# Attention and two MLP blocks on one core: heads on all rows of the array, fewer load issues, a new list of steps, weight subtractions on VectorE

## Chip, cores and metric

One core of a Trainium2 chip. The metric is the device time of one execution in microseconds (us), lower is better. Engines by their names in the profile: PE = TensorE matmul, PEld = its weight loads, DVE = VectorE, ACT = ScalarE, POOL = GpSimd, SP = SyncE; SPq is the queue on which SP issues transfers (DMA).

## What is computed

Windowed attention (batch 4, 8 heads, 576 tokens, head size 64; heads 0 to 3 see the last 32 tokens, heads 4 to 7 every fourth of the last 128), then two MLP blocks over 2304 tokens of width 512. All is float32.

```python
scores = q @ k.T / sqrt(64); scores = where(mask, scores, -1e9)
attn = exp(scores - max); attn = attn / (sum(attn) + 1e-9)
x = attn @ v                                  # then to [2304, 512]
h = x @ w_in;  x = (h - tanh(h)) @ w_out      # w_in [512, 2048], w_out [2048, 512]
out = ((x @ w1) * (x @ w2)) @ w3 @ w_out2     # w1, w2 [512, 1024], w3 [1024, 1024], w_out2 [1024, 512]
```

## The kernel before

**Attention.** The work is cut into 12 units (a batch and a third of its tokens) and two types of heads, plain (p) and dilated (d), whose tokens the host has put into residue order so that both types use the same narrow windows. A type of a unit is a part here, so there are 24. A part has two pairs of heads (e) and three blocks of 64 tokens (i). Each part goes through these steps, named by one letter in the list:

- q: load of k and q (`load_q`, L295). k is one issue (L306); q is four issues (L313), one for each pair and head, each the 64 rows of one head. The type takes one half of the 128 rows (`r`).
- v: load of v (`load_v`, L322, L333), 2 issues or, for the first third of a batch, 4.
- s: scores (`at_scores`, L371). A matmul of identity and mask opens the bank (L389); then 24 matmuls of 64 rows, 32 columns of weights (q) and 64 moving columns (k) add to it (L402), each two instructions in the trace. The four column strips of the array are two heads by two halves of a block. Units 0 to 2 run one type at a time; from unit 3 on `s3` and its like run both, each on its half of the rows.
- M, E, N, m: maximum and subtraction (DVE), exponential (ACT), sum and reciprocal (DVE), product (POOL).
- T: three transposes by PE (L447); C: their copy to SBUF (ACT, L455).
- P: weighted sum of v (`at_pv`, L458, L476): 24 matmuls of 64 rows by 64 weight columns and 32 moving columns.
- X, L: the high part of the result on ACT (L498) and the rest on DVE (L503), written to X.

**First block.** A float32 product is computed from high and low parts by three matmuls. Its 16 chunks of 128 hidden columns are in four groups of 3, 4, 4 and 5. Steps: h (`st_h`: x @ w_in), t, g, G, k (tanh, subtraction, high, low), y (`st_y`: product with w_out), Y, Z (to SBUF). A step of 256 tokens has 12 matmuls for h and 12 for y. The first group runs beside the attention, in the order that `ORDER` (L45) writes out by hand for all engines at once: every engine and SP's queue get their instructions in the order of the words, and wait in that order. `S5` is five matmuls on zeros. The words h0 to h24 are the steps of h; h24 is the first of group 1, from where loops give the order.

**Weights** arrive as 64-bit words and are turned into float32 high and low parts: w (load, `load64`), a (L126, ACT), b and c (L131, L135, L141, L144, DVE), i (high, `cv_hi`, ACT), o (low, `cv_lo`, L152, POOL). Outside the list `tick` (L188) does this for one weight; `need` calls it until a weight is there; two staging buffers hold arriving words. Converted weights take free slots (`free`), which `release` and `settle` give back two steps later.

**Second block.** First `WW` = w3 @ w_out2, 8 steps of 24 matmuls (L739). Then for tiles of 512 tokens and 8 chunks j: `st_ab` (two products of 12 matmuls each, pa and pb; a_sb from pa by ACT, L777; the product with pb by DVE, L778; cs high by ACT, L780, cs low by DVE, L781), and `st_out` of the step before (L797, 12 matmuls that need cs). In the first tile every step calls `tick` twice after `st_ab`. `y_split` (L726) makes the high and low parts of the next tile's input, on ACT and DVE.

Of the kernel before, what the change touches and what calls it, by code (L numbers as in the profile page):

```python
# [50 lines left out]
t2 C3p q5 g2 i4 b5 T3d G2 o4 h3 c5 C3d k2 P3 M4 i5 t3 q6 o5 y1 X3p X3d L3p E4 L3d y2 N4 s5 Y2 Z2 m4p
v5d g3 m4d G3 T4p v5p M5 k3 h4 C4p q7 T4d E5 s6 C4d N5 t4 P4 g4 m5p M6 G4 q8 y3 m5d X4p X4d k4 T5p
L4p E6 L4d s7 C5p N6 v6p T5d m6p h5 C5d M7 m6d q9 T6p t5 P5 g5 E7 s8 X5d N7 X5p G5 C6p k5 L5p v7d y4
L5d m7d v7p m7p T6d w6 h6 C6d M8 w7 T7p t6 y5 g6 E8 q10 G6 N8 a6 h7 k6 Y5 Z5 C7p m8p s9 a7 b6 m8d t7
v6d g7 T7d c6 G7 h8 k7 C7d q11 M9 i6 T8p t8 o6 y6 g8 E9 b7 y7 G8 N9 k8 w8 h9 c7 m9d m9p P6 t9 w9 i7
g9 y8 X6p o7 X6d v8p L6p C8p L6d h10 G9 v8d Z8 Y8 k9 a8 y9 a9 b8 t10 c8 P7 s10 b9 X7p w10 X7d L7p
g10 v9d T8d L7d G10 h11 c9 k10 C8d v9p M10 P8 t11 a10 w11 y10 X8d X8p L8d v10p E10 g11 s11 L8p G11
v10d N10 k11 h12 b10 m10p c10 m10d y11 t12 g12 w12 T9p Z11 G12 h13 Y11 k12 C9p y12 t13 g13 G13 T9d
k13 h14 C9d M11 P9 t14 g14 E11 T10p v11p h15 X9p N11 C10p v11d G14 X9d k14 T10d L9p t15 y13 L9d m11p
C10d g15 m11d P10 G15 k15 h16 X10p X10d L10p L10d T11p t16 y14 g16 C11p T11d Z14 G16 h17 Y14 k16  # L60
C11d y15 t17 g17 P11 G17 k17 y16 X11p X11d L11p L11d Q0 h18 i8 i9 o8 y17 t18 i10 g18 o9 G18 a11 h19
# [7 lines left out]
def attn_moe_kernel(  # L69
# [276 lines left out]
    def banks_of(n, ty):  # L346

        if n >= PB:
            s = ust[n]
            return s["both"][:, ty], lambda: s["xt"][:, ty]  # L350
        m = order0.index((n, ty))
        if 2 <= m < 4:

            ps = yA.tile([128, 2, 256], F32, tag=f"y{m - 2}", name=f"s{m}").rearrange("p a c -> p (a c)")
        else:
            if m % 4 == 0:
                banks0["s"] = attn_pools["psS"].tile([128, 2, 512], F32, tag="s", name="s")
            ps = banks0["s"][:, m % 2]

        def x():  # L360
            if m % 2 == 0:
# [542 lines left out]
```

## Time and profile before

| | us |
|---|---|
| median of 3 runs | 870.97 |
| lowest, highest | 868.84, 871.27 |
| the profiled execution | 869.45 |
| its span, first to last instruction | 867.7 |

| engine | busy us | share of the span |
|---|---|---|
| PE | 825.8 | 95% |
| PEld | 693.8 | 80% |
| DVE | 430.1 | 50% |
| ACT | 277.9 | 32% |
| POOL | 139.2 | 16% |

The shares are means over stages that differ; the section of rows below splits the span into stages. The clock of a row is the share of full speed that TensorE was granted: 1.00 is 2.4 GHz, 0.50 is 1.2 GHz. A busy PE is not always PE at its peak, since a matmul counts as busy from its start to its modelled end.

### The profile page before, as it was taken

The numbers are of one execution on the slowest core, as the hardware profiler recorded it, in microseconds if no ns is written. First come the engines' busy times: TensorE is split into PE (matmuls) and PEld (weight loads), VectorE is DVE, ScalarE is ACT, GpSimd is POOL, SyncE is SP. The second block draws the span as 40 slices with busy tenths as digits, with TensorE's granted clock in tenths as the row PEclk, the third lists the DMA queues.
The fourth block names the chain that finished last, engine by engine and source line by source line (L and its number), as shares of the span: only waits on it lengthen the run. The fifth ranks groups of instructions, "written<-read, shape, count | busy, mean of one in ns | idle before, by whom it ended". The sixth has DMA issues, their size and how long they took to land.

```text
span 867.7 us, 14652 instructions
## 1 busy us (share of the span) xinstructions
PE 825.8 (95%) x6153; PEld 693.8 (80%) x6153; DVE 430.1 (50%) x728; ACT 277.9 (32%) x507; POOL 139.2 (16%) x136
## 2 busy tenths in 40 slices
PE   7878859999999999999999999999899999999998
PEld 3577658988888988888888898887688888888897
DVE  4566447465763576335776776766722222222121
ACT  2333234544432243223444433334321121121121
POOL 3232222351210021001222211222100000000000
PEclk9588969999999999999999999999999999999999
DMA  6675567121220022002232222323010010010010
GB/s 155 176 215 130 124 174 229 43 74 48 97 74 1 25 97 74 1 1 67 89 103 98 96 83 74 104 91 122 25 49 1 1 48 1 1 49 0 1 49 25
DMA packets 49250, 63.18 MB, mean 73 GB/s; under 512 B 23072, under 2 KB 37536, under 8 KB 49184
## 3 DMA queue, kind: packets, MB, share of 16 engines
q1 hardware_dynamic: 48896, 61.88, 23.7%
q8 instruction: 48, 0.79, 0.4%
q10 hardware_dynamic: 288, 0.36, 0.2%
q14 instruction: 18, 0.15, 0.1%
HBM read 57.51 MB, written 4.72 MB: 72 GB/s over the span
## 4 chain that ended last, share of the span: by engine, by line
PE 79%; SPq 7%; DMA 5%; DVE 4%; ACT 2%; issue 2%; POOL 0%; ACTq 0%; DVEq 0%; POOLq 0%
PE h L519 46%; PE y L609 21%; PE o L797 10%; SPq L313 4%; SPq L333 2%; DMA st<-in_w 2%; PE x L476 1%; SPq L306 1%; DMA st<-in_w_out 1%; DMA st<-in_w_in 1%; DMA v<-in_vt 1%; DMA Y<-in_kT 1%; DVE a L141 1%; DVE a L135 1%; DVE a L144 1%
## 5 line engine op out<-in xcount | busy, mean ns | idle before, releaser
L609 PE MATMUL y<-gs,WG 128*128 128x512 f32 (+1 forms) x648 | 125.3, 342 | 0.1
L519 PE MATMUL h<-X,WG 128*128 128x256 f32 (+1 forms) x591 | 122.6, 343 | 1.9 <-DVE th L567 1.9
L519 PE MATMUL h<-X,LT 128*128 128x512 f32 (+1 forms) x552 | 122.1, 368 | 0.0
L567 DVE TENSOR_TENSOR th<-h,th 128x512 f32<-128x512 f32 (+1 forms) x83 | 51.3, 618 | 131.1 <-ACT th L561 130.9
L519 PE MATMUL h<-LT,X 128*128 128x512 f32 (+1 forms) x402 | 115.9, 373 | 0.0
L609 PEld LDWEIGHTS y<-gs,WG 128*128 128x128 f32 x648 | 104.2, 194 | 13.3 <-POOL gs L581 0.3
L519 PEld LDWEIGHTS h<-X,LT 128*128 128x128 f32 x552 | 96.7, 189 | 17.3
L519 PEld LDWEIGHTS h<-X,WG 128*128 128x128 f32 x591 | 95.9, 198 | 13.7 <-DVE th L567 2.5
L778 DVE TENSOR_TENSOR a_sb<-h,a_sb 128x512 f32<-128x512 f32 (+1 forms) x40 | 25.5, 637 | 158.7 <-PE h L519 152.4
L609 PE MATMUL y<-gs,LT 128*128 128x512 f32 (+1 forms) x420 | 93.4, 368 | 0.9 <-DVE gs L581 0.9
L561 ACT ACTIVATE th<-h 128x512 f32<-128x512 f32 (+1 forms) x83 | 44.8, 540 | 137.7 <-PE h L519 137.6
L609 PEld LDWEIGHTS y<-gs,LT 128*128 128x128 f32 x420 | 74.1, 188 | 14.1 <-DVE gs L581 1.1
L519 PEld LDWEIGHTS h<-LT,X 128*128 128x128 f32 x402 | 73.5, 188 | 13.3
L519 PE MATMUL h<-WG,X 128*128 128x512 f32 (+1 forms) x225 | 69.2, 375 | 0.0
L574 ACT ACTIVATE gs<-th 128x512 fp32r<-128x512 f32 (+1 forms) x83 | 47.8, 576 | 60.7 <-DVE th L567 56.7
L141 DVE SCALAR_TENSOR_TENSOR a<-st,a 128x512 uint32<-128x512 uint32 x72 | 60.4, 839 | 2.2
L126 ACT ACTIVATE a<-st 128x512 f32<-128x512 f32 x72 | 47.8, 664 | 41.9 <-DMA st<-in_w_in 20.2
L152 POOL TENSOR_TENSOR WG<-a,WG 128x512 fp32r<-128x512 f32 x27 | 35.1, 1298 | 141.0 <-ACT WG L149 125.6
L144 DVE SCALAR_TENSOR_TENSOR a<-st,a 128x512 uint32<-128x512 uint32 x72 | 54.0, 750 | 2.5
L797 PE MATMUL o<-X,cs 128*128 128x512 f32 x216 | 52.6, 391 | 1.9 <-ACT cs L780 1.9
L777 ACT ACTIVATE a_sb<-h 128x512 f32<-128x512 f32 (+1 forms) x40 | 22.0, 551 | 94.2 <-PE h L519 94.2
L780 ACT ACTIVATE cs<-a_sb 128x512 fp32r<-128x512 f32 (+1 forms) x40 | 23.6, 589 | 87.9 <-DVE a_sb L778 87.9
(84 smaller groups left out, 1013.2 us busy)
## 6 DMA issues: line engine op xcount, KB each, us to landing
st<-in_w SPq DMA_DIRECT2D x32, 512.0 KB, 3.3
st<-in_w_in SPq DMA_DIRECT2D x16, 512.0 KB, 3.5
st<-in_w_out SPq DMA_DIRECT2D x16, 512.0 KB, 3.6
v<-in_vt SPq DMA_DIRECT2D x28, 192.0 KB, 3.8
st<-in_wo SPq DMA_DIRECT2D x8, 512.0 KB, 3.2
q<-in_qz SPq DMA_DIRECT2D x72, 48.0 KB, 2.9
k<-in_kT SPq DMA_DIRECT2D x12, 224.0 KB, 3.8
v<-in_vt SPq DMA_DIRECT2D x14, 128.0 KB, 3.8
```

Source lines behind the costliest of these rows:

```text
L126: nc.scalar.activation(out=a.bitcast(F32), in_=st[:, :, 1].bitcast(F32), func=ACTF.Abs)
L141: nc.vector.scalar_tensor_tensor(out=a, in0=st[:, :, 1], scalar=0xC0000000, in1=a, op0=ALU.bitwise_and, op1=ALU.bitwise_or)
L144: nc.vector.scalar_tensor_tensor(out=a, in0=st[:, :, 0], scalar=29, in1=a, op0=ALU.logical_shift_right, op1=ALU.bitwise_or)
L152: nc.gpsimd.tensor_tensor(out=lo, in0=a.bitcast(F32), in1=hi.bitcast(F32), op=ALU.subtract)
L313: nc.sync.dma_start(out=q[r, e, h], in_=qz[b, 2 * ty + e, D * h:D * h + D, TU * g:TU * g + TU, QT * h:QT * h + QT],)
L519: nc.tensor.matmul(out=ps, lhsT=a[sel[0]], rhs=b[sel[1]], start=(start and i == 0), stop=(i == n - 1), **kw)
L561: nc.scalar.activation(out=th[:, :tn], in_=gst[i][:, :tn], func=ACTF.Tanh)
L567: nc.vector.tensor_tensor(out=th[:, :tn], in0=ps[:, :tn], in1=th[:, :tn], op=ALU.subtract)
L574: nc.scalar.activation(out=gs[:, 0, :tn], in_=th[:, :tn], func=ACTF.Copy)
L609: nc.tensor.matmul(out=y[k], lhsT=wt[sel[0]][:, 128 * k:128 * k + 128], rhs=gs[:, sel[1], tn * m:tn * m + tn], start=(cs[m] == 0 and n == ...
L778: nc.vector.tensor_tensor(out=a_sb[:, :tn], in0=pb[:, :tn], in1=a_sb[:, :tn], op=ALU.mult)
L797: nc.tensor.matmul(out=ps, lhsT=cs[:, e, 128 * m:128 * m + 128], rhs=WW[j][f], start=(j == 0 and n == 0), stop=(j == NJ - 1 and n == 2),)
```

## The change

- Loads: a part has its own k and q tiles on all 128 rows, one issue for each. q is now loaded with its zero blocks (128 rows: one head's rows hold q, the other's zeros, in the columns of each head), 384 KB instead of four times 48 KB. Three buffers for k and q (before, two of a whole unit), three for v (four).
- Scores: 24 matmuls a part of 128 rows, 32 weight columns, 64 moving columns; the four column strips as before, no half of rows for a type any more.
- C: the transposed weights go to a tile `pb` that holds blocks on a diagonal (pair e in rows 64 e and on), in two ACT instructions of 64 rows; its zeros are written once by two POOL memsets at the start.
- P: 12 matmuls a part of 128 rows (both pairs), 64 weight columns, 64 moving columns. Its PSUM tile is one bank, two buffers (before, one of two banks).
- A new list for the first group; q, v and P come by part everywhere. M, E and N stay for both types at once from unit 3 on.
- From WW on (`late`), the low part of weights is computed by DVE; a weight's steps are spread around the evacuation in `st_ab`; WW takes one or two weights a step; in the first tile, two weights in the first two steps, then one. `y_split` is cut in two (`y_hi`, `y_lo`).

```diff
--- before.py
+++ after.py
-q0p S10 v2p K0 q2p K1 s0p w0 S5 M0p q1p E0p s2p N0p q0d S3 a0 m0p M2p T0p b0 E2p q1d C0p s1p N2p c0
-m2p S1 v0p s0d M1p i0 w2 S1 o0 M0d E1p s1d v1p N1p E0d P0p w1 M1d m1p S1 X0p a2 T1p q2d L0p N0d S3
...
+q0p S10 q1p K0 K1 q1d s0p S2 M0p q2p s1p E0p N0p S6 v1p M1p m0p T0p E1p q0d S1 C0p N1p s2p m1p v0p
+M2p T1p S4 C1p q2d E2p s0d N2p s1d m2p v0d M0d P0p E0d M1d w0 P1p X0p N0d E1d T2p w1 X1p N1d m0d s2d
+C2p L1p m1d L0p T0d v2p M2d a0 S5 C0d v1d b0 E2d T1d c0 a1 q3p S2 P2p N2d i0 P0d o0 b1 X2p w2 C1d S6
+X0d q3d L2p m2d L0d P1d c1 T2d X1d v2d a2 L1d i1 b2 h0 C2d w3 o1 c2 s3 t0 q4p g0 i2 P2d M3 G0 o2 q4d
+a3 h1 X2d k0 b3 E3 y0 w4 t1 c3 v3p g1 i3 s4 L2d G1 o3 N3 v3d a4 k1 h2 M4 w5 m3p m3d T3p t2 v4p g2
+C3p b4 h3 G2 q5p c4 E4 P3p t3 a5 g3 k2 T3d N4 X3p v4d h4 i4 C3d o4 L3p q5d b5 t4 P3d y1 g4 m4d X3d
+c5 v5p h5 G3 q6p L3d m4p i5 s5 k3 o5 t5 w6 g5 T4p M5 y2 q6d C4p P4p Y2 Z2 E5 q7p T4d y3 C4d N5 X4p
+v5d P4d G4 m5p L4p G5 a6 m5d T5p v6p X4d b6 s6 C5p k5 c6 w7 T5d P5p M6 k4 q7d C5d y4 X5p i6 L5p E6
...
-        nc.gpsimd.tensor_tensor(out=lo, in0=a.bitcast(F32), in1=hi.bitcast(F32), op=ALU.subtract)
+        (nc.vector if late else nc.gpsimd).tensor_tensor(out=lo, in0=a.bitcast(F32), in1=hi.bitcast(F32), op=ALU.subtract)
...
+    def conv_bits():
+        if absed and len(free) - (reserve[0] if absed[0][0][0] in ("w1", "w2") else 0) >= 2:
+            key, st, a = absed.popleft()
+            cv_bits(st, a)
+            late[0] = key, a, free.popleft(), free.popleft()
+        prefetch()
+        if loaded and not absed:
+            key, st = loaded.popleft()
+            absed.append((key, st, cv_abs(st)))
+
+    def conv_hi():
+        if late[0]:
+            cv_hi(late[0][1], late[0][2])
+
+    def conv_lo():
+        if late[0]:
+            key, a, hi, lo = late[0]
+            cv_lo(a, hi, lo)
+            W[key] = (hi, lo)
+            late[0] = None
+
+    def tick_late():
+
+
+        conv_lo()
+        conv_bits()
+        conv_hi()
+
...
-                tick()
+                tick_late() if late else tick()
...
-        attn_pools["kv"] = st.enter_context(tc.tile_pool(name="kv", bufs=2))
-        attn_pools["vv"] = st.enter_context(tc.tile_pool(name="vv", bufs=4))
+        attn_pools["kv"] = st.enter_context(tc.tile_pool(name="kv", bufs=3))
+        attn_pools["vv"] = st.enter_context(tc.tile_pool(name="vv", bufs=3))
...
-        attn_pools["pt"] = st.enter_context(tc.tile_pool(name="pt", bufs=4))
+        one = st.enter_context(tc.tile_pool(name="att", bufs=1))
+        attn_pools["pb"] = one.tile([128, NPB, TU, 4, 2, HQ], F32, name="pb")
...
-        attn_pools["psX"] = st.enter_context(tc.tile_pool(name="psX", bufs=1, space=PSUM))
+        attn_pools["psX"] = st.enter_context(tc.tile_pool(name="psX", bufs=2, space=PSUM))
+
+        for e in range(2):
+            nc.gpsimd.memset(attn_pools["pb"][64 * e:64 * e + 64, :, :, :, 1 - e], 0.0)
...
-            if n not in ks:
-                k = home(n, 4 * WK, "kv", "k").rearrange("p (m k) -> p m k", m=4)
...
             for ty in parts:
-                r = slice(64 * ty, 64 * ty + 64)
+                k = home(n, 2 * WK, "kv", "k").rearrange("p (e k) -> p e k", e=2)
+                q = home(n, 2 * TU * 2 * QT, "kv", "q").rearrange("p (e t c) -> p e t c", e=2, t=TU)
                 nc.sync.dma_start(
-                    out=k[r, :, :k1 - k0],
-                    in_=kT[b, 2 * ty:2 * ty + 2, :, k0:k1].rearrange("e (h p) k -> p (e h) k", h=2),
+                    out=k[:, :, :k1 - k0], in_=kT[b, 2 * ty:2 * ty + 2, :, k0:k1].rearrange("e p k -> p e k")
                 )
-                for m in range(4):
-                    e, h = divmod(m, 2)
-
-                    nc.sync.dma_start(
-                        out=q[r, e, h],
-                        in_=qz[b, 2 * ty + e, D * h:D * h + D, TU * g:TU * g + TU, QT * h:QT * h + QT],
-                    )
+                nc.sync.dma_start(
+                    out=q, in_=qz[b, 2 * ty:2 * ty + 2, :, TU * g:TU * g + TU].rearrange("e p t c -> p e t c")
+                )
+                ks[n, ty] = k, q
...
-        for i in range(TU):
-            t = TU * g + i
-            for e in range(2):
-                for ty in parts:
-                    r = slice(64 * ty, 64 * ty + 64)
+        for ty in parts:
+            k, q = ks.pop((n, ty))
+            for i in range(TU):
+                t = TU * g + i
+                for e in range(2):
                     for j in range(4):
-                        h, half = divmod(j, 2)
-                        k0 = KS[t] - KS[TU * g] + window(t, half)
+                        k0 = KS[t] - KS[TU * g] + window(t, j % 2)
                         nc.tensor.matmul(
-                            out=ps[ty][HQ * j:HQ * j + HQ, 2 * i + e],
-                            lhsT=q[r, e, h, i, HQ * half:HQ * half + HQ],
-                            rhs=k[r, 2 * e + h, k0:k0 + HW], start=False, stop=(i == TU - 1),
-                            skip_group_check=True, tile_position=(64 * ty, HQ * j),
+                            out=ps[ty][HQ * j:HQ * j + HQ, 2 * i + e], lhsT=q[:, e, i, HQ * j:HQ * j + HQ],
+                            rhs=k[:, e, k0:k0 + HW], start=False, stop=(i == TU - 1),
+                            skip_group_check=True, tile_position=(0, HQ * j),
                         )
...
-            pt = attn_pools["pt"].tile([128, TU, 128], F32, tag="p", name="p")
-            nc.scalar.activation(out=pt, in_=ust[n]["pt"][u], func=ACTF.Copy)
-            ust[n]["pt"][u] = pt
+            pt = ust[n]["pt"][u]
+            pb = ust[n]["pt"][u] = attn_pools["pb"][:, npb[0] % NPB]
+            npb[0] += 1
+            for e in range(2):
+                nc.scalar.activation(
+                    out=pb[64 * e:64 * e + 64, :, :, e],
+                    in_=pt[64 * e:64 * e + 64].rearrange("p i (j q) -> p i j q", j=4), func=ACTF.Copy,
+                )
...
-                for half in range(2):
-                    for e in range(2):
-                        for h in range(2):
-                            dst = x[64 * h:64 * h + 64, e]
-                            if ty:
-                                dst = dst[:, QT * i + HQ * half:QT * i + HQ * half + HQ]
-                            else:
...
-                            j = 2 * h + half
-                            nc.tensor.matmul(
-                                out=dst, lhsT=v[64 * e:64 * e + 64, half, i, D * h:D * h + D],
-                                rhs=s["pt"][ty][64 * e:64 * e + 64, i, HQ * j:HQ * j + HQ],
-                                start=True, stop=True, tile_position=(64 * e, 64 * h),
-                            )
+                for half, h in ((0, 0), (0, 1), (1, 0), (1, 1)):
+                    dst = x[64 * h:64 * h + 64]
+                    if ty:
+                        dst = dst[:, :, QT * i + HQ * half:QT * i + HQ * half + HQ]
+                    else:
+
+                        dst = dst.rearrange("p e (r c l) -> p c e l r", r=R, l=HQ // R)[:, 2 * i + half]
+                    nc.tensor.matmul(
+                        out=dst, lhsT=v[:, half, i, D * h:D * h + D],
+                        rhs=s["pt"][ty][:, i, 2 * h + half].rearrange("p a q -> p (a q)"), start=True, stop=True,
+                    )
+            s["x"][ty] = x
...
-        def y_split(t, k):
+        def y_hi(t, k):
             t0, tn = tiles[t]
-            ysp.setdefault(t, [])
             hi, lo = free.popleft(), free.popleft()
             nc.scalar.activation(out=hi[:, :tn], in_=Y[:, k, t0:t0 + tn], func=ACTF.Copy)
+            ysp.setdefault(t, []).append((hi, lo))
+
+        def y_lo(t, k):
+            t0, tn = tiles[t]
+            hi, lo = ysp[t][k]
             nc.vector.tensor_tensor(
                 out=lo[:, :tn], in0=Y[:, k, t0:t0 + tn], in1=hi[:, :tn].bitcast(F32), op=ALU.subtract
             )
-            ysp[t].append((hi, lo))
...
+        while bitsed:
+            split()
+        late.append(None)
...
             hi, lo = free.popleft(), free.popleft()
+            tick_late()
+            if i % 2:
+                tick_late()
             nc.scalar.activation(out=hi, in_=ps, func=ACTF.Copy)
-            tick()
...
+            if 2 <= i <= 5:
+                y_lo(0, i - 2)
             if 1 <= i <= 4:
-                y_split(0, i - 1)
+                y_hi(0, i - 1)
...
+            ny = j - 3 if 3 <= j < 7 and t + 1 < len(tiles) else None
+            if ny is not None:
+                y_hi(t + 1, ny)
+            conv_lo()
+            if t == 0:
+                conv_bits()
+            if ny is not None:
+                y_lo(t + 1, ny)
             a_sb = act_p.tile([128, 512], F32, tag="th", name="a_sb")
             nc.scalar.activation(out=a_sb[:, :tn], in_=pa[:, :tn], func=ACTF.Copy)
+            conv_hi()
             nc.vector.tensor_tensor(out=a_sb[:, :tn], in0=pb[:, :tn], in1=a_sb[:, :tn], op=ALU.mult)
             cs = spl_p.tile([128, 2, 512], F32R, tag="gs", name="cs")
             nc.scalar.activation(out=cs[:, 0, :tn], in_=a_sb[:, :tn], func=ACTF.Copy)
+            conv_lo()
             nc.vector.tensor_tensor(
                 out=cs[:, 1, :tn], in0=a_sb[:, :tn], in1=cs[:, 0, :tn].bitcast(F32), op=ALU.subtract
             )
+            if t == 0 and j < SECOND:
+                conv_bits()
+                conv_hi()
...
-                t, j = steps2[i]
-                if t == 0:
-                    tick()
-                    tick()
-                if j >= 3 and j < 7 and t + 1 < len(tiles):
-                    y_split(t + 1, j - 3)
...
```

## Rows read from the trace of the kernel before

**Rows 1.** Windows by stage: length, busy us of each engine (instructions), granted clock, DMA.
```profile
core 0: us, PE busy (x) PEld busy (x) DVE busy (x) ACT busy (x) POOL busy (x), PEclk, DMA share, GB/s
0.00:47.01 47.01, 37.28 (x684) 22.83 (x684) 23.25 (x54) 12.47 (x24) 12.68 (x25) 0.71 0.65 171
47.01:125.35 78.34, 57.10 (x1165) 50.70 (x1164) 43.55 (x75) 26.40 (x56) 22.46 (x25) 0.80 0.63 160
125.35:195.20 69.85, 67.90 (x1156) 62.78 (x1155) 40.06 (x72) 32.84 (x75) 27.82 (x29) 0.98 0.38 115
195.20:519.33 324.13, 323.26 (x1573) 273.81 (x1572) 194.48 (x335) 120.68 (x199) 50.74 (x40) 1.00 0.19 63
...
570.00:620.00 50.00, 46.11 (x200) 36.76 (x198) 37.18 (x54) 18.82 (x32) 12.90 (x10) 1.00 0.28 95
```

**Rows 2.** Waits of PE, 0 to 125 us: total, times, longest (us).
```profile
PE t L447 <- ACT p L455: 8.9, 3, 7.1
PE s L402 <- DMA q<-in_qz: 7.7, 10, 2.2
```

**Rows 3.** Chain that ended last, 0 to 118 us, by line.
```profile
by line: SPq L313 29.5%; SPq L333 14.7%; SPq L306 7.4%; DMA st<-in_w_out 6.3%; DMA st<-in_w_in 6.1%; DMA v<-in_vt 5.3%; DMA Y<-in_kT 5.3%; PE h L519 5.1%; issue 4.6%; DMA q<-in_qz 4.0%; PE x L476 2.9%; PE s L402 2.5%; SPq L121 2.5%; PE y L6
```

**Rows 4.** Time line of SP's queue: start, us, engine, line, issues.
```profile
62.58 0.61 SPq L306 DMA_DIRECT2D k<-in_kT  x1
63.23 3.33 SPq L313 DMA_DIRECT2D q<-in_qz  x4
```

**Rows 5.** DMA issues: count, KB each, us to landing.
```profile
v<-in_vt SPq DMA_DIRECT2D x28, 192.0 KB, 3.8
...
q<-in_qz SPq DMA_DIRECT2D x72, 48.0 KB, 2.9
```

**Rows 6.** Windows: scores of one type, of two; P of two; dense DMA.
```profile
15.90:17.10 1.20, 1.20 (x48) 0.99 (x48) 1.15 (x1) 0.02 (x1) 0.60 (x1) 1.00 0.23 55
...
61.65:62.80 1.15, 1.15 (x97) 1.09 (x96) 1.11 (x4) 1.12 (x3) 0.12 (x1) 1.00 0.64 186
...
126.90:128.40 1.50, 1.50 (x97) 1.46 (x96) 0.42 (x1) 0.90 (x2) 1.23 (x3) 1.00 0.58 163
26.00:30.00 4.00, 3.41 (x35) 1.91 (x35) 1.72 (x5) 1.93 (x4) 0.83 (x1) 0.50 0.98 304
```

**Rows 7.** Unit steps: chain at 152 us, mask matmuls, copy (x24, mean 487 ns).
```profile
152.87 0.33 PE t L447 x3
153.19 1.43 PE h L519 x12
...
61.23 0.49 PE L389 MATMUL s<-mask_sb,id_sb 128*128 128x384 bf16 x2
...
L455 ACT ACTIVATE p<-t 128x384 f32<-128x384 f32 x24 | 11.7, 487 | 16.1 <-PE t L447 16.1
```

**Rows 8.** First matmuls of h0, h9 (time line of PE) and h24 (chain).
```profile
47.01 1.67 PE L519 MATMUL h<-X,WG 128*128 128x256 f32 x12
...
125.35 1.60 PE L519 MATMUL h<-X,WG 128*128 128x256 f32 x12
...
195.20 2.72 PE h L519 x12
```

**Rows 9.** First tile of second block: PE's waits; DVE and POOL time lines.
```profile
PE o L797 <- ACT cs L780: 3.9, 2, 2.0
...
570.59 0.42 DVE L131 TENSOR_SCALAR a<-a 128x512 f32<-128x512 f32 x1
...
572.84 0.42 DVE L131 TENSOR_SCALAR a<-a 128x512 f32<-128x512 f32 x1
...
573.75 1.81 DVE L141 SCALAR_TENSOR_TENSOR a<-st,a 128x512 uint32<-128x512 uint32 x1
...
573.72 1.29 POOL L152 TENSOR_TENSOR X<-a,X 128x512 fp32r<-128x512 f32 x1 [7.55 <-ACT X L149]
...
502.11 0.69 DVE L581 TENSOR_TENSOR gs<-th,gs 128x512 fp32r<-128x512 f32 x1
```

More of the change, by code (lines that the diff above doesn't have):

```diff
@@ L16 @@
 PH = 1
+SECOND = 2
 GS = (3, 4, 4, 5)
@@ L51 @@
[L51 to L61, printed above, removed]
@@ new lines @@
+w8 o6 L4d h6 a7 N6 q8p y5 t6 b7 g6 m6d s7 c7 G6 Y5 v6d a8 Z5 k6 i7 w9 h7 b8 M7 m6p y6 q8d t7 o7 g7
+E7 T6p c8 h8 q9p G7 a9 N7 k7 C6p P5d t8 w10 b9 s8 X5d m7d L5d g8 v7p m7p c9 G8 y7 q9d k8 T6d a10 P6p
+C6d M8 q10p h9 X6p L6p E8 y8 b10 v7d t9 g9 P6d N8 G9 w11 Y8 k9 s9 X6d Z8 m8d L6d v8p m8p c10 T7p
+q10d h10 C7p P7p t10 q11p g10 T7d G10 X7p h11 k10 M9 C7d v8d T8p t11 P7d g11 E9 w12 L7p s10 X7d N9
+C8p v9p L7d m9p P8p m9d q11d T8d X8p y9 C8d L8p M10 v9d h12 G11 k11 E10 P8d t12 N10 s11 X8d v10p L8d
@@ new lines @@
+m10p g12 m10d h13 y10 t13 g13 y11 G12 k12 T9p Y11 Z11 h14 C9p G13 T9d k13 t14 y12 g14 C9d M11 y13
+G14 k14 E11 P9p N11 P9d X9p v10d L9p m11p T10p X9d h15 v11p C10p L9d m11d T10d t15 P10p g15 C10d y14
+X10p v11d G15 L10p k15 P10d Y14 Z14 T11p X10d h16 C11p L10d y15 t16 g16 G16 P11p k16 h17 X11p L11p
+y16 t17 g17 G17 h18 k17 y17 t18 g18 G18 T11d k18 Y17 Z17 h19 C11d P11d t19 g19 y18 X11d G19 L11d Q0
+k19 i8 h20 i9 o8 i10 y19 t20 o10 a11 g20 G20 b11 h21 k20 c11 y20 o9 t21 w13 i11 g21 o11 G21 h22 Z20
@@ L65 @@
+a12 Y20 k21 b12 a13 y21 t22 b13 g22 c12 G22 h23 k22 c13 i12 y22 t23 o12 i13 g23 G23 o13 h24 k23 y23
+t24 g24 G24 k24 Y23 Z23
 """
@@ L172, in attn_moe_kernel @@
     reserve = [0]
+    late = []
     loaded = deque()
@@ L226, in attn_moe_kernel @@
     AB = (0, 1)
+    NPB = 2
     Yf = Y.rearrange("p k n -> p (k n)")
@@ L344, in attn_moe_kernel, with bank_of @@
     banks0 = {}
-    def banks_of(n, ty):
+    def bank_of(n, ty):
         if n >= PB:
-            s = ust[n]
-            return s["both"][:, ty], lambda: s["xt"][:, ty]
+            return ust[n]["both"][:, ty]
         m = order0.index((n, ty))
         if 2 <= m < 4:
-            ps = yA.tile([128, 2, 256], F32, tag=f"y{m - 2}", name=f"s{m}").rearrange("p a c -> p (a c)")
-        else:
[L356 to L361, printed above, removed]
-                banks0["x"] = x_tile()
-            return banks0["x"][:, m % 2]
-        return ps, x
-    def x_tile():
-        x = attn_pools["psX"].tile([128, 2, 512], F32, tag="x", name="x")[:, :, :2 * TU * QT]
-        return x.rearrange("p e (u c) -> p u e c", u=2)
+            return yA.tile([128, 2, 256], F32, tag=f"y{m - 2}", name=f"s{m}").rearrange("p a c -> p (a c)")
+        if m % 4 == 0:
+            banks0["s"] = attn_pools["psS"].tile([128, 2, 512], F32, tag="s", name="s")
+        return banks0["s"][:, m % 2]
     def at_scores(n, parts=AB):
         b, g = units[n]
-        k, q = ks[n]
         if n not in ust:
@@ L380, in at_scores @@
                 pm = attn_pools["pp"].tile([128, 2, NB, HW], F32, tag="pm", name="pm")
-            ust[n] = dict(mx=ms[:, 0], sm=ms[:, 1], pm=pm, ps={}, pt={}, x={}, left=2)
+            ust[n] = dict(mx=ms[:, 0], sm=ms[:, 1], pm=pm, ps={}, pt={}, x={})
             if n >= PB:
@@ L385, in at_scores @@
         for ty in parts:
-            bank, ust[n]["x", ty] = banks_of(n, ty)
-            ps[ty] = bank[:, :NB * HW].rearrange("p (i k) -> p i k", i=NB)
+            ps[ty] = bank_of(n, ty)[:, :NB * HW].rearrange("p (i k) -> p i k", i=NB)
             m0 = (M_DIL if ty else M_PLAIN)[g]
@@ L458, in at_pv @@
     def at_pv(n, parts=AB):
         s = ust[n]
-        if n >= PB:
-            s["xt"] = x_tile()
         for ty in parts:
-            x = s["x"][ty] = s["x", ty]()
+            x = attn_pools["psX"].tile([128, 2, TU * QT], F32, tag="x", name="x")
             v = vs.pop((n, ty))
             for i in range(TU):
-                for half in range(2):
-                    for e in range(2):
-                        for h in range(2):
-                            dst = x[64 * h:64 * h + 64, e]
-                            if ty:
-                                dst = dst[:, QT * i + HQ * half:QT * i + HQ * half + HQ]
-                            else:
-                                dst = dst.rearrange("p (r c l) -> p c l r", r=R, l=HQ // R)[:, 2 * i + half]
-                            j = 2 * h + half
-                            nc.tensor.matmul(
-                                out=dst, lhsT=v[64 * e:64 * e + 64, half, i, D * h:D * h + D],
-                                rhs=s["pt"][ty][64 * e:64 * e + 64, i, HQ * j:HQ * j + HQ],
-                                start=True, stop=True, tile_position=(64 * e, 64 * h),
-                            )
+                for half, h in ((0, 0), (0, 1), (1, 0), (1, 1)):
[8 more added lines that the diff above has]
+                    )
```

10 lines of the change are left out of this document (1 added, 9 removed).

## The prediction

> **What bounds the kernel now.** I read the stages first. From 195 us to 570 us PE is busy without a gap at the full clock, and no edit shortens its work there; the first 125 us are different: PE is busy 37.3 of 47.0 us and 57.1 of 78.3 us, at a mean clock of 0.71 and 0.80 [rows 1]. So the question is what PE waits for there. The waits name loads of q and a transpose behind a late step [rows 2]; the chain of the first 118 us names the issuing queue: SP, issuing q (L313), v (L333) and k (L306), carries 29.5, 14.7 and 7.4% of it, PE's own lines little [rows 3]. In the queue's time line one q of one head type is four issues in 3.33 us, and the k issue before it is followed by it without a pause [rows 4]. An issue costs about 0.65 us with its gap (0.61 for one; from 62.58 to 63.23). The code makes 96 issues of q, 24 of k, 64 of v and 14 of weights in the first group: 198 x 0.65 = 129 us of queue. The tokens of the list before h0 hold 42.2 us of these issues, and h0 starts at 47.0; after h9, at 125.35, only 16 us of issues are left, and PE is busy 67.9 of 69.85 us [rows 1, 8]. So until h9 SP's queue sets the pace, then PE.
>
> **Loads.** q goes from four issues to one per unit and type: 96 to 24, which takes 72 x 0.65 = 47 us off the queue (129 to 82). The bytes of q double, since its zero blocks are now loaded as well: 4 x 48 KB becomes 384 KB [rows 5], or 4.7 MB more in all, 31.4 MB instead of 26.7 by the end of the first group. DMA moved 171 and 160 GB/s at shares of 0.65 and 0.63 in the two stretches [rows 1], which is 257 GB/s at a full share; in a stretch at 0.98 it moved 304 [rows 6]. The old q moves in 256-byte pieces and the new one in 1536-byte pieces, as v does. So I take 300 GB/s where DMA is the limit, with 257 as the near bound and 230 as a bad one.
>
> **Scores.** Before, units 0 to 2 run one type at a time, on half the rows: 48 instructions in 1.20 us. Later units run both types at once, on both halves: 97 in 1.15 us, so 12 ns each instead of 25 [rows 6]. After the change one type takes all rows, and the four column tiles are all that can run side by side. The nearest row is the one with four tiles: 25 ns, 1.20 us for a type. That is no change for the first six parts (a part is one unit and one type) and 0.6 us more for each of the other 18: **+10.8 us of PE**. Below, 12 ns would be no cost; above, see the first rival. The mask matmul costs 0.42 for two (from 61.23 to the scores at 61.65), 0.21 for a part [rows 6, 7].
>
> **Weighted sum (P).** Before, a part is 48 instructions of 32 columns on four tiles: 97 in 1.50 us for two parts, so 0.77 with the gap [rows 6]. After, it is 24 instructions of 64 columns on two tiles. No row shows this form. If the two tiles overlap fully, half the columns of a transposed 128-column block (0.33 us for three, so 110 ns, 55 for 64 columns [rows 7]), shared by two, gives 27 ns and 0.65 us; if they do not, 55 ns and 1.32 us. I take 0.96, between them, as the score rows show tiles that overlap in part: **+0.19 a part, +4.6 us** in all, with -2.9 and +13 as ends.
>
> **Copies and clearing.** The copy of the transposed block becomes two ACT instructions of 64 partitions, each as long as the old one (487 ns [rows 7]): +11.7 us on ACT, which is busy 26.4 of 78.3 and 32.8 of 69.9 us [rows 1], so it hides; uncovered it would add 0.5 us to a part's chain. Two memsets on POOL come ahead of the first mask copies; at worst 1.29 us each, as POOL's longest kind [rows 9]; the first loads of k and q cover them, and without that cover they cost 2.6 us once.
>
> **The sum of the first group.** Unit costs: h or y step 1.44 us, the three 512-wide ones 2.72 [rows 7, 8]; transposes 0.33, scores with mask 1.41, P 0.96 a part. Before, the list from h9 to h24 adds up to 64.4 us of PE work at these prices (scores of two parts 1.63, P 0.77) and took 69.85, from 125.35 to 195.20 [rows 8]: a factor of 1.085 where PE sets the pace.
> After, start to h0: the list's issues before h0 are 22.8 us, its PE work 23.0 with spins, and the loads that h0 needs are the first 7.0 MB, 23.5 us at 300 GB/s. With landing (about 4 us) and the last part's P, copies and subtraction that makes 31; in-order waits on the way add, as 42.2 became 47.0 before: **35 us**, ends 31 and 42.
> From h0 to h24: 18 parts of scores 25.4, 18 of transposes 5.9, 19 of P 18.2, h 38.4, y 35.7: 123.6 us, times 1.085 = 134. The loads between h0 and h12 are 20.5 MB, 68 us at 300 GB/s and 80 at 257, beside PE work of 69.8 x 1.085 = 76 us: both nearly full, with three buffers for k and q, so some loads will be late and the clock will fall after a few waits. I add 5 us. h24 starts at 35 + 139 = **174 us** instead of 195.2: **-21 us**.
> From h0 to h24 VectorE was busy 43.6 + 40.1 = 84 us, ACT 59, POOL 50 [rows 1]; the same work (ACT 68 with the second copies) in 139 us leaves each of them room, so none is next.
>
> **Groups 1 to 3** (195 to 519) run from code that does not change until WW begins: 0.
>
> **Last weights.** PE waits 3.9 us in two places in the first tile of the second block, for cs [rows 9]. There every step converted two weights: one takes VectorE 2.25 us (570.59 to 572.84), the next one longer, as L141 takes 1.81 us while POOL's 1.29 us subtraction (L152) runs [rows 9]; VectorE is busy 37.2 of 50 us [rows 1]. After, the subtraction costs VectorE about 0.69 (its like, L581 [rows 9]), so 2.94 us a weight; POOL is silent, and L141 should keep its fast form. Counting free slots by the code, WW still converts five of the 16 tiles of w1 and w2; the first two steps then convert two each, four steps one, and step 6 three, forced by need. A one-weight step holds 2.94 + 3 x 0.69 (product, cs, Y) = 5 us of VectorE work against a PE period of 8.16 (36 instructions, 12 of them 2.72 [rows 8]). At step 6 the forced tile is queued behind cs of step 5 and is ready about as pb needs it. I take **-3.5 us**, ends -3.9 and +1. At worst its two instructions on ACT and VectorE push pb back by 1 us. In WW, eight conversions (23.5) and twelve subtractions (8.3) are 32 us of VectorE in 43.5 of PE: covered.
>
> **Total:** -21 - 3.5 = -24.4 with roundings. The profiled run took 869.45 (span 867.7), 1.5 below the median of 870.97: 845.1 there, **847 us** against the median.
>
> **Rivals.**
> *The column tiles stop overlapping (slower).* On all rows every load of weights meets rows in use. If a part's instructions then run one by one, scores cost 48 x 55 ns = 2.64 and P 1.32 us a part: +1.8 us on 18 parts, 32.4 x 1.085 = 35 us. h24 comes at 209, +14 us against before; less 3.5: 881 us. It decides above 24.4 / 1.085 / 18 = 1.25 us a part. For it: new instructions all share one row group. Against: the single-type rows share one row group, too, and run at 25 ns. The Trainium skill, "TensorE: Matmul & The Clock Gate", section "Part 3: Packing small matmuls — row/col tiling", says that a load of weights overlaps matmuls in flight only where the row group differs; by that rule this rival is what happens, and the trace speaks against it in the 25 ns of [rows 6], where the row group is one and the columns differ. Chance 0.09.
> *DMA takes the queue's place.* If it moves 230 GB/s, h12 comes at 35 + 89 = 124, and 54 x 1.085 = 59 more gives 183: -12 - 3.5, **856 us**. For it: 257 GB/s at a full share in the old mix; against: 304 in a dense stretch. Chance 0.2.
> *One big load costs the queue what four did.* Each q issue 2.6 us: 24 x 1.95 = 47 us back on SP, the pace of before and more PE work behind it: about 870. Against it: a k issue (192 or 224 KB by the code) costs 0.61, an issue of q with 48 KB no less [rows 4, 5]. Chance 0.04.
> *PE keeps 12 ns and P 0.65.* The list's work from h0 falls by 16 us, DMA sets the pace to h12: h24 at about 160, **833 us**. Chance 0.09.
>
> **Numbers.** The forecast has 0.58, within 839 to 855. The range takes in the DMA rival and most of the faster one: 832 to 865. About 0.3% (2.6 us) is what a measurement can tell from no change. Faster: 0.58 + 0.2 + 0.09 = 0.87; same 0.04; slower 0.09.
>
> **What would show it.** SP: 24 issues of q, with pauses. h0 near 35, h24 near 174. Scores of one part 1.2 us, P 0.96. DMA share above 0.9 up to h12. PE without the two waits for cs; L141 near 0.69 us all through the last weights. It would be wrong if scores ran above 50 ns an instruction, or if h0 stayed above 42.

## The result

| | median us | lowest, highest | runs |
|---|---|---|---|
| before | 870.66 | 868.84, 871.27 | 4 |
| after | 832.87 | 830.28, 833.35 | 4 |

The ratio is 0.9563, with a 95% interval of 0.9538 to 0.9588: the changed kernel is 37.8 us faster. The forecast of 847 was 14 us too slow. The time lies outside the band 839 to 855, which had most of the chance, and under 1 us inside the lower end of the range, 832; the kernel's own runs spread over 3 us, so that it lies inside is luck. It falls on the 833 of the fastest rival, though not by that rival's way, as the step-by-step section below tells. The profiled execution took 830.28, its span is 828.5.

The windows of the kernel after, cut at the same steps as [rows 1]: start to h0, h0 to h24, h24 to the first product of WW. Two shorter ones follow: 54 us from the first `st_out`, and from the first to the last one. Columns as in [rows 1].

```profile
0.00:33.29 33.29, 25.27 (x463) 15.53 (x469) 21.02 (x48) 13.01 (x25) 11.32 (x25) 0.90 0.94 277
33.29:160.89 127.60, 119.12 (x1960) 107.11 (x1958) 91.27 (x151) 71.47 (x154) 51.74 (x54) 1.00 0.64 184
160.89:485.30 324.41, 323.54 (x1574) 274.08 (x1573) 194.65 (x335) 121.54 (x200) 52.48 (x41) 1.00 0.20 64
539.61:593.61 54.00, 54.00 (x240) 44.64 (x239) 37.48 (x64) 20.44 (x35) 0.00 (x0) 1.00 0.25 78
539.61:821.21 281.60, 281.60 (x1333) 236.98 (x1332) 87.95 (x146) 65.53 (x118) 0.00 (x0) 1.00 0.10 31
```

h0 starts at 33.29 instead of 47.01 and h24 at 160.89 instead of 195.20 [rows 8]: 34.3 of the 39.2 us between the spans are there. The third stretch is the one that nothing touches, and it is as long as before (324.13 in [rows 1]). From the first to the last `st_out` before took 286.73 us, after 281.60: 5.1 us. The rest agrees within 0.3.

In the first stretch DMA has a share of 0.94, where it had 0.65; the granted clock is 0.90 and then 1.00, where it was 0.71, then 0.80 up to h9 and 0.98 behind it. PE's waits in the kernel after, 0 to 170 us (total, times, longest), against [rows 2]:

```profile
PE s L412 <- DMA q<-in_qz: 3.9, 3, 2.3
PE h L530 <- DVE th L578: 2.7, 2, 2.3
PE t L456 <- issue: 1.9, 1, 1.9
PE s L412 <- DMA Y<-in_qz: 1.5, 3, 1.1
```

and in SP's time line one part's k and q are now two issues, against 0.61 and 3.33 us in [rows 4]:

```profile
36.42 0.37 SPq L336 DMA_DIRECT2D k<-in_kT  x1
36.83 0.47 SPq L339 DMA_DIRECT2D q<-in_qz  x1
```

### The profile page after: what moved, and what is told of

It reads as the page before. It is cut to its first block, busy times and chain, and to the rows that moved or that the text cites. A ratio compares the mean times of both kernels' runs of the same rounds, so it can differ in the third digit from the quotient of the medians.

```text
span 828.5 us, 13467 instructions
## 1 busy us (share of the span) xinstructions
PE 806.8 (97%) x5575; PEld 680.7 (82%) x5580; DVE 433.4 (52%) x747; ACT 292.8 (35%) x531; POOL 115.8 (14%) x119
## 4 chain that ended last, share of the span: by engine, by line
PE 88%; DMA 6%; DVE 3%; SPq 1%; issue 1%; ACT 0%; ACTq 0%; DVEq 0%
PE h L530 51%; PE y L620 22%; PE o L831 12%; DMA q<-in_qz 3%; DMA Y<-in_qz 2%; DMA v<-in_vt 2%; PE x L487 2%; SPq L359 1%; DMA st<-in_w_out 1%; PE t L456 1%; DVE a L143 1%; DVE a L146 0%; PE s L412 0%; DVE a L137 0%; DVE a L133 0%
## 5 line engine op out<-in xcount | busy, mean ns | idle before, releaser
L530 PE MATMUL h<-X,LT 128*128 128x512 f32 (+1 forms) x687 | 164.9, 370 | 0.0
L530 PEld LDWEIGHTS h<-X,LT 128*128 128x128 f32 x687 | 122.1, 188 | 22.1
L530 PE MATMUL h<-X,WG 128*128 128x256 f32 (+1 forms) x600 | 119.6, 337 | 3.0 <-DVE th L578 2.7
L620 PEld LDWEIGHTS y<-gs,WG 128*128 128x128 f32 x648 | 102.1, 189 | 13.7 <-POOL gs L592 0.5
L530 PE MATMUL h<-LT,X 128*128 128x512 f32 (+1 forms) x210 | 67.0, 368 | 0.0
L831 PE MATMUL o<-X,cs 128*128 128x512 f32 x270 | 65.3, 390 | 0.0
L530 PE MATMUL h<-X 128*128 128x512 f32 (+1 forms) x189 | 61.7, 377 | 0.0
L831 PEld LDWEIGHTS o<-X,cs 128*128 128x128 f32 x270 | 50.4, 188 | 10.2
L530 PE MATMUL h<-WG,X 128*128 128x512 f32 (+1 forms) x189 | 57.7, 377 | 0.0
L143 DVE SCALAR_TENSOR_TENSOR a<-st,a 128x512 uint32<-128x512 uint32 x72 | 54.1, 752 | 2.2
L146 DVE SCALAR_TENSOR_TENSOR a<-st,a 128x512 uint32<-128x512 uint32 x72 | 52.3, 726 | 2.5
```

What stands on the lines that cost most here:

```text
L143: nc.vector.scalar_tensor_tensor(out=a, in0=st[:, :, 1], scalar=0xC0000000, in1=a, op0=ALU.bitwise_and, op1=ALU.bitwise_or)
L146: nc.vector.scalar_tensor_tensor(out=a, in0=st[:, :, 0], scalar=29, in1=a, op0=ALU.logical_shift_right, op1=ALU.bitwise_or)
L530: nc.tensor.matmul(out=ps, lhsT=a[sel[0]], rhs=b[sel[1]], start=(start and i == 0), stop=(i == n - 1), **kw)
L620: nc.tensor.matmul(out=y[k], lhsT=wt[sel[0]][:, 128 * k:128 * k + 128], rhs=gs[:, sel[1], tn * m:tn * m + tn], start=(cs[m] == 0 and n == ...
L831: nc.tensor.matmul(out=ps, lhsT=cs[:, e, 128 * m:128 * m + 128], rhs=WW[j][f], start=(j == 0 and n == 0), stop=(j == NJ - 1 and n == 2),)
```

## The experiments

Each was timed beside runs of the kernel before. "After" is the changed kernel, 832.87 us.

### The queue: four issues again, and one issue in the kernel before

**e1_q_four.** After, with q of a part in four issues of the same bytes and pieces.

```diff
-                nc.sync.dma_start(out=q, in_=qz[b, 2 * ty:2 * ty + 2, :, ...])
+                for m in range(4):
+                    e, h = divmod(m, 2)
+                    nc.sync.dma_start(
+                        out=q[64 * h:64 * h + 64, e],
+                        in_=qz[b, 2 * ty + e, D * h:D * h + D, TU * g:TU * g + TU],
+                    )
```

> The changed kernel, but q of a part again in four issues (a half of the rows and one pair each): the same bytes, the same pieces of 1536 bytes, 72 issues more. Queue theory (SP's issues paced the first 125 us before): the issues before h12 go from 76 to 123 us (24 x 3 x 0.65 more), so h12 comes near 125 instead of 105 and the kernel takes 845 to 856 us. Rival (the larger pieces made the gain): h12 stays near 105 and the time within 3 us of 833.

Measured: 854.39 us (853.03 to 857.00), ratio 0.9849 (0.9829 to 0.9868). PE's waits in the first 170 us and the first matmuls of h0:

```profile
PE s L415 <- DMA q<-in_qz: 12.7, 10, 5.1
40.67 1.92 PE L533 MATMUL h<-X,WG 128*128 128x256 f32 x12
```

The same bytes in 72 more issues cost 21.5 us, of which 7.4 come before h0. The waits for q go from 3.9 to 12.7 us.

**e5_before_q_one.** The kernel before, its list and scores as they were, with q of a part in one issue (192 KB, no zero blocks).

```diff
-                for m in range(4):
-                    e, h = divmod(m, 2)
-                    nc.sync.dma_start(out=q[r, e, h], in_=qz[b, 2 * ty + e, D * h:D * h + D, ...])
+                nc.sync.dma_start(
+                    out=q[r].rearrange("p e h t c -> p (e h) (t c)"),
+                    in_=qz[b, ty, :, :, TU * g:TU * g + TU].rearrange("d m t c -> d m (t c)"),
+                )
```

> The kernel before with one change: q of a part comes with one issue instead of four (the host lays out the same blocks for it, 192 KB, no zero blocks). Queue theory: SP's issues of the first group fall from 129 to 82 us, with the old list and the old scores; h0 comes near 38 instead of 47, h9 near 100 instead of 125, and the kernel takes 843 to 852 us. Rival (the old list or its scores set the pace as much as the queue): 860 us or more.

Measured: 843.71 us (839.85 to 844.73), before 869.08 beside it, ratio 0.9715 (0.9691 to 0.9738). One edit alone brings 25 of the 38 us. In its trace h24 (L516 here) starts 30.5 us earlier than in [rows 8]:

```profile
164.73 1.52 PE L516 MATMUL h<-X,WG 128*128 128x512 f32 x6
```

Both directions agree: the gain hangs on the number of issues. (e5 also makes the pieces of q longer; e1 keeps them as they are.) That was the first step of the prediction.

**e3_q_packed.** After, but the host packs q without zero blocks, still one issue (192 KB instead of 384), and the scores use only the 64 rows that hold q.

```diff
-    out=ps[ty][...], lhsT=q[:, e, i, HQ * j:HQ * j + HQ], rhs=k[:, e, k0:k0 + HW], tile_position=(0, HQ * j),
+    out=ps[ty][...], lhsT=q[64 * (j // 2):64 * (j // 2) + 64, e, i, HQ * (j % 2):HQ * (j % 2) + HQ],
+    rhs=k[64 * (j // 2):64 * (j // 2) + 64, e, k0:k0 + HW], tile_position=(64 * (j // 2), HQ * j),
```

> As e2, and q is laid out by the host without its zero blocks, so one issue of a part brings 192 KB instead of 384 KB: 4.7 MB less in the first 110 us. DMA theory (after the change DMA at a share of 0.94 sets the pace to h12): h0 comes at 28 to 30 instead of 33.3, h12 near 95 instead of 105, time 822 to 828 us, less what e2 shows scores on 64 rows to cost. Rival (PE sets the pace all through): as e2.

Measured: 825.86 us (823.83 to 826.68), ratio 0.9507 (0.9491 to 0.9522), 7 us below after. The first 110 us, after's row first, then that of this kernel:

```profile
0.00:110.00 110.00, 94.76 (x1921) 76.49 (x1926) 86.68 (x157) 57.84 (x119) 43.80 (x60) 0.97 0.93 270
```
```profile
0.00:110.00 110.00, 97.33 (x1988) 79.53 (x1994) 86.56 (x158) 58.04 (x120) 44.50 (x60) 0.98 0.81 234
```

At 270 GB/s DMA was nearly full in the changed kernel (0.93); with 4.7 MB less its share falls to 0.81, no wait of PE for q is listed, and h24 comes at 156.51. So the added bytes cost 4.4 us up to h24 in these traces and 7 in the medians. From h0 to h12, though, the two traces take equally long:

```profile
33.29:105.30 72.01, 65.80 (x1376) 57.96 (x1374) 62.35 (x103) 42.81 (x91) 30.86 (x32) 1.00 0.94 271
```
```profile
31.23:103.24 72.01, 66.82 (x1376) 58.90 (x1374) 62.93 (x104) 42.68 (x91) 30.85 (x32) 0.98 0.81 234
```

2.1 of the 4.4 us lie before h0, and 2.3 between h12 and h13, where PE of the changed kernel waits 2.3 us for one q. The DMA theory got its time, but not its marks: h0 came at 31.23 (expected 28 to 30) and h12 at 103.24 (expected near 95). So DMA made loads late in places, but did not set the pace to h12. One trace of each kernel tells no more: from h0 to h12, e4 below takes 76.43 us with the loads of after, and e10 69.58 with those of e3.

### The scores: rows, sharing, and the wrong row

**e2_s_rows64.** After, with the scores on only the 64 rows that hold q; the loads stay.

```diff
-    lhsT=q[:, e, i, HQ * j:HQ * j + HQ], rhs=k[:, e, k0:k0 + HW], tile_position=(0, HQ * j),
+    lhsT=q[64 * (j // 2):64 * (j // 2) + 64, e, i, HQ * j:HQ * j + HQ],
+    rhs=k[64 * (j // 2):64 * (j // 2) + 64, e, k0:k0 + HW], tile_position=(64 * (j // 2), HQ * j),
```

> The changed kernel, but a score matmul takes only the 64 rows that hold q (the zero rows are loaded and not used); the four column tiles then lie two on each half of the rows. Tile theory (a 64-row tile takes about 100 ns an instruction however many run beside it, four at once make 25 ns): 48 instructions take 1.2 us instead of 0.8, PE's work grows by 8 to 10 us, the time is 836 to 843 us. Rival (25 ns before came from all four tiles sharing one half of the rows): with two halves in turn 0.6 to 0.8 us a part, 833 us. Clock theory (all rows in use keep the clock up): the granted clock of the first 160 us falls below 0.9.

Measured: 831.57 us (829.67 to 837.03), ratio 0.9586 (0.9551 to 0.9621): as after. The granted clock of the first 160 us is 0.98 in both, so the clock theory falls.

**e7_s_onehalf.** After, with all four column tiles on rows 0 to 63, so that the second head of each pair meets only the zeros.

```diff
-    lhsT=q[:, e, i, HQ * j:HQ * j + HQ], rhs=k[:, e, k0:k0 + HW], tile_position=(0, HQ * j),
+    lhsT=q[0:64, e, i, HQ * j:HQ * j + HQ], rhs=k[0:64, e, k0:k0 + HW], tile_position=(0, HQ * j),
```

> The changed kernel, but all four score matmuls of a block use rows 0 to 63 alone (half of the heads get the zero rows, so their scores are left out; timing only). Sharing theory (25 ns an instruction comes from four tiles on one half of the rows): 48 instructions take 1.2 us instead of 0.8, as single types did before; PE's work grows by up to 10 us and the time by 3 to 9 us, to 836 to 842. Rival (25 ns came from something else in the first 20 us before, such as data that still arrived): 0.8 us and 833.

Measured: 828.53 us (828.01 to 835.28), ratio 0.9554 (0.9514 to 0.9594): not told apart from after. Scores in the time line of after (128 rows), of e2 (64 rows on both halves) and of e7 (one half); start, us, shape, count:

```profile
56.36 0.88 PE L412 MATMUL s<-k,q 128*32 128x64 f32 x48
65.69 1.55 PE L412 MATMUL s<-k,q 128*32 128x64 f32 x96
```
```profile
56.02 1.54 PE L412 MATMUL s<-k,q 64*32 64x64 f32 x96
```
```profile
32.83 0.88 PE L412 MATMUL s<-k,q 64*32 64x64 f32 x48
55.64 1.54 PE L412 MATMUL s<-k,q 64*32 64x64 f32 x96
```

These spans include the last instruction's own duration; start to start, 96 take 1.47 to 1.48 us. Four column tiles run at 15 to 17 ns an instruction, with 64 rows or 128, on one half or both. So neither the number of rows nor the sharing of a row half made the 25 ns of [rows 6], and both theories for it fall. What did shows when that 1.20-us row is cut up. The weight loads (PEld) of the scores in the kernel before; busy time and instructions, then clock, DMA share and GB/s:

```profile
15.88:16.06 0.18, 0.14 (x4) 1.00 0.19 53
16.06:16.24 0.18, 0.14 (x4) 1.00 0.49 122
16.24:16.42 0.18, 0.14 (x4) 1.00 0.37 88
16.42:16.98 0.56, 0.55 (x36) 1.00 0.14 30
```

The first twelve come in three groups of four, 0.18 us apart; the other 36 follow within 0.56 us, at the rate of the other kernels. In e5, with the same 64-row form of a single type, but one load of q instead of four, the group takes 0.80, evenly (PE, scores alone):

```profile
9.86:10.26 0.40, 0.40 (x29) 1.00 0.96 348
10.26:10.66 0.40, 0.40 (x35) 1.00 1.13 293
```

The row that I priced from holds waits and was no price. The cause is in the trace: the first instructions of the four groups each wait for another of the part's four loads of q, and these land at 15.84, 16.02, 16.20 and 16.39 us; each group starts 0.04 us behind its load. Such short waits (below 0.2 us) do not stand in the list of waits.

### The list

**e6_old_list.** After, with the list of before. That list makes up to two further copies (C) before the P of a part, and only two buffers for the copied block are left, so some parts' sums are made from another part's block; its time is that of an order of work only.

```diff
-ORDER = """ (list of after) """
+ORDER = """ (list of before) """
```

> The changed kernel with the list of the kernel before. What e1 leaves of the first group's gain (34 us, of which e1 gives back about 23) should hang on the list: 842 to 852 us. Rival (the list is only fitted to the loads, any order near it does): within 4 us of 833.

Measured: 858.66 us (856.56 to 866.13), ratio 0.9891 (0.9856 to 0.9926), 26 us above after, and above the 842 to 852 that I expected. PE's waits, 0 to 130 us:

```profile
PE h L529 <- DVE th L577: 11.7, 2, 10.6
PE s L411 <- DMA q<-in_qz: 8.4, 4, 4.4
PE x L486 <- DMA v<-in_vt: 7.4, 3, 3.8
```

the longest of VectorE and ACT, 100 to 130 us, and those of SP's queue before issues of k and v, 0 to 130 us:

```profile
DVE a L132 <- ACT a L127: 12.6, 1, 12.6
ACT a L127 <- DMA st<-in_w_in: 13.0, 1, 13.0
SPq L335 <- PE s L411: 21.9, 5, 10.9
SPq L358 <- PE x L486: 20.0, 5, 10.1
```

One wait of 10.6 us is for VectorE, which itself waited 12.6 us for ACT's first step of a weight's conversion, and ACT 13.0 us for that weight's load. That load was issued late, at 119.16, since SP's queue stood: the issue of k ahead of it had waited 10.9 us for PE's scores to free a buffer. In all the queue waited 41.9 us for PE's scores and sums. The new buffers (three for v and for k, two for the copies) need the new list. This doesn't make the list worth 26 us by itself: with its own buffers the old list gave 843.71 in e5.

### The last weights

**e4_late_old.** After, with WW and the second block as before.

```diff
-            tick_late()
-            if i % 2:
-                tick_late()
             nc.scalar.activation(out=hi, in_=ps, func=ACTF.Copy)
+            tick()
...
+                if t == 0:
+                    tick()
+                    tick()
```

> The changed kernel with WW and the second block as before: low parts of weights on POOL, two weights a step in the first tile, Y parts in one piece. My step: the two waits for cs, 3.9 us, come back; time 836.5 to 838 us. Rival (more of the last 5 us than these waits hangs on it): 840 us and above; or nothing: 833.

Measured: 838.31 us (833.96 to 840.16), ratio 0.9646 (0.9614 to 0.9679), 5.4 above after, between the two times expected. The waits for cs are back, three in its trace:

```profile
PE o L808 <- ACT cs L791: 5.0, 3, 2.3
```

**e8_late_pool.** After, with the low parts on GpSimd again, the rest of the late order new.

```diff
-        (nc.vector if late else nc.gpsimd).tensor_tensor(out=lo, ...)
+        nc.gpsimd.tensor_tensor(out=lo, ...)
```

> The changed kernel, new order of the late weights, but their low parts on POOL as before. Engine theory (POOL's subtraction slows VectorE's L143 to 1.8 us, and that made cs late): PE's waits for cs come back at least in part, 835 to 839 us. Order theory (one weight a step and the split of Y's parts are enough): no wait, 833 us, though L143 is slow again in places.

Measured: 830.54 us (829.53 to 831.26), ratio 0.9558 (0.9540 to 0.9577): no loss. The conversion's L143 in the late part, of after and then of e8 (mean ns):

```profile
L143 DVE SCALAR_TENSOR_TENSOR a<-st,a 128x512 uint32<-128x512 uint32 x19 | 13.2, 692 | 0.7
```
```profile
L143 DVE SCALAR_TENSOR_TENSOR a<-st,a 128x512 uint32<-128x512 uint32 x19 | 19.6, 1033 | 0.7
L154 POOL TENSOR_TENSOR X<-a,X 128x512 fp32r<-128x512 f32 x8 | 10.3, 1291 | 35.4 <-ACT X L151 35.4
```

L143 is slow again (1033 instead of 692 ns), yet PE has no wait for cs. The move to VectorE, which the change is named for, brings nothing.

**e9_two_a_step.** After, but each step of the first tile converts two weights behind its own work, as before did.

```diff
-            conv_lo()
-            if t == 0:
-                conv_bits()
...
                 st_ab(i)
+                if steps2[i][0] == 0:
+                    tick_late()
+                    tick_late()
```

> The changed kernel with one thing undone: in the first tile of the second block every step converts two weights again, one after the other behind the step's own work, instead of one or two spread between the step's parts. The subtraction stays on VectorE and the WW stretch stays new. Pacing theory (the late gain is the spreading of the conversions): the product and the rounding of cs queue behind two conversions of about 3 us each, PE waits for cs again, some 4 to 6 us in two or three places, and the time is 836 to 839 us. WW theory (the gain is in how the WW stretch is ordered and in the split of Y in two steps): PE does not wait for cs, and the time stays at 832 to 834.

Measured: 840.15 us (839.06 to 840.85), ratio 0.9664 (0.9646 to 0.9683), 7.3 above after. PE's waits in the second block, and the three steps of `st_out` behind them (start and length of their 12 matmuls, 2.88 us where nothing waits; the wait in brackets):

```profile
PE o L823 <- ACT cs L806: 5.2, 3, 2.2
566.97 4.66 PE L823 MATMUL o<-WG,cs 128*128 128x512 f32 x12 [2.14 <-ACT cs L806]
577.88 3.29 PE L823 MATMUL o<-X,cs 128*128 128x512 f32 x12 [0.81 <-ACT cs L806]
588.83 3.29 PE L823 MATMUL o<-X,cs 128*128 128x512 f32 x12 [2.22 <-ACT cs L806]
```

Pacing theory holds: undoing the spreading alone loses the whole late gain. (The spreading is two things, fewer weights a step and their place between the step's parts; no run tells them apart.) The 5.2 us of waits cost 8.6 us from the first to the last `st_out` (290.2 against 281.6). The 12 matmuls behind each wait take 3.29 us instead of 2.88 since there is a second wait among them: the weight loads of PE (PEld) wait for the low part of cs, which VectorE finishes after ACT's high part. This happens in four places, since the step at 556.12, whose high part came just in time, has it too. e9's line, then that of the kernel before:

```profile
PEld o L823 <- DVE cs L807: 1.7, 4, 0.4
```
```profile
PEld o L797 <- DVE cs L781: 1.1, 3, 0.4
```

So about 6.9 of the 8.6 us are waits for cs, and 1.4 more went to the 12 matmuls that took 4.66 us at a lower clock.

### The two edits together

**e10_packed_pool.** e3 with the low parts on GpSimd.

```diff
-        (nc.vector if late else nc.gpsimd).tensor_tensor(out=lo, ...)
+        nc.gpsimd.tensor_tensor(out=lo, ...)
```

> The changed kernel with the two edits that did not lose: q without its zero blocks in one load of 192 KB per unit and type, with the scores on the 64 rows that hold q, and the low parts of the last weights on GpSimd as before. If the two are independent, the time is that of the packed q less one or two microseconds: 823 to 826 us. If the slower form of the VectorE conversions beside GpSimd costs anything, it is above 826.

Measured: 823.96 us (823.04 to 824.79), ratio 0.9480 (0.9462 to 0.9498): the fastest here, 8.9 us below after, though not told apart from e3, whose runs overlap it.

## Why it came out so, step by step

- **What bounds (right).** SP's issues set the pace up to h9: e1 and e5 show it from both sides, at 21.5 and 25 us for 72 issues, 0.30 and 0.35 us each in the end time, out of the 0.65 that an issue holds the queue. The prediction turned 47 us of queue time into 21 of gain at h24, since it expected PE and DMA to take over at the prices below; with PE cheaper and DMA not setting the pace, 34.3 were gained.
- **Start to h0 (right).** 35 predicted, 33.29 measured; DMA moved 277 GB/s at a share of 0.94, against 300 taken and 257 as the near bound.
- **Scores (the step that failed).** 1.20 us a part taken from one row; measured 0.80 alone and 0.74 in pairs, from 48 and 96 instructions. 18 parts by 0.4 is 7.2 us, 7.8 with the factor of 1.085. The lower end, 12 ns, was named, but as no cost and not as the likelier case.
- **Weighted sum (right in kind, 2 us too dear).** 0.96 taken; 24 instructions start at 48.53 and the next work at 49.38, so 0.85, 35 ns each, between the ends of 27 and 55:

```profile
48.53 0.92 PE L487 MATMUL x<-pb,v 128*64 128x64 f32 x24
49.38 0.55 PE L456 MATMUL t<-id_sb,pm 128*128 128x128 f32 x3
```

- **h0 to h24.** 123.6 us of work less 7.2 and 2.1 is 114.3; times 1.085 it is 124, and with the 5 us that were added for late loads 129. Measured 127.60. So the shape of the sum held and the two prices explain 10 of the 11.4 us.
- **Late loads and the clock (half right).** Some loads of q were late (3.9 + 1.5 us), and e3 puts their cost at 4.4 us up to h24, 2.3 of them behind h0. The clock did not fall after them: it is 1.00 from h0 to h24. So the 5 us that were added for both stood for about half as much.
- **Copies and clearing (right).** Two copies of 483 ns a block and two clearings of 734 ns are there, and ACT is busy 71.5 of 127.6 us; PE waits 0.5 us in all for a copy.

```profile
L469 ACT ACTIVATE pb<-t 64x384 f32<-64x384 f32 x38 | 18.4, 483 | 9.2 <-PE t L456 8.7
L277 POOL MEMSET pb<- 64x768 f32 x2 | 1.5, 734 | 0.1
```

- **Groups 1 to 3 (right).** 0 predicted, +0.3 measured.
- **Last weights (too small, reason half wrong).** -3.5 predicted, with -3.9 as the far end; -5.1 measured; both waits for cs are gone and L143 stays at 692 ns. But the prediction gave the fast form of L143 a part in it, and e8 shows that it has none: the spreading does it (e9). Beyond the 3.9 us of waits for the high part of cs, the kernel before loses 1.1 us to waits for its low part (the line of PEld under e9), and the sum left these out: 5.0 of the 5.1.
- **The rivals.** Column tiles that run one by one (881 us): fell, at 15 to 17 ns an instruction. The rule of the Trainium skill, "TensorE: Matmul & The Clock Gate", "Part 3: Packing small matmuls — row/col tiling", that a load of weights overlaps matmuls in flight only where the row group differs, is not borne out here: after has one row group and e2 two, and both need 1.5 us for 96. Big loads that hold the queue like four issues (870): fell, at 0.47 us for 384 KB. DMA at 230 GB/s (856): fell, at 270, though loads of q were late in places. PE at the old rate with DMA at its limit (833): its time came out, but not its way. Scores ran at 15 to 17 ns instead of 12, P cost 0.85 us instead of 0.65, and DMA did not set the pace to h12 (e3); that the sums meet at 833 is chance.

That P on two halves of the rows might run faster still wasn't tried.

## What to carry to other kernels

Count the issues on a queue, not only the bytes: where the chain of waits names the queue, merging four small loads into one was worth 25 us here even before anything else changed. The zero blocks that the changed kernel's one load brings with it then cost 7 us. Before a price is taken from a single row, cut the row in two: if its halves do not hold the same number of instructions, look for a wait in it, in the weight loads too. Work for a later stage that shares engines with a pipelined step goes between the step's parts, in small portions; which engine does it can matter less.

## What the runs showed of the chip that was not expected

- Matmuls of 32 weight columns and 64 moving columns in float32, on four column strips, cost the same with 64 rows as with 128, on one row half or two: 0.88 us for 48 and 1.54 to 1.55 for 96. Only eight tiles, four column strips on each half of the rows, as the two types had before, were faster (97 in 1.15 us [rows 6]).
- A wait of 2.1 us in the second block was followed once by a fall of the clock and once not: in e9 the 12 matmuls behind the wait at 566.97 took 4.66 us at a granted clock of 0.63, those behind the equally long one at 588.83 took 3.29 at a clock of 1.00.

```profile
566.97:571.60 4.63, 4.63 (x13) 3.45 (x14) 3.83 (x7) 1.24 (x2) 0.00 (x0) 0.63 0.07 6
```
